# Attention and a two-branch MoE layer on one core: engines ordered by hand, scores in two groups a head pair, q and k loaded as rows of 2 KB

## The chip, the cores and the metric

The kernel runs on one core of a Trainium2 chip. That core has a matrix engine (TensorE, PE in the profile, with its weight loads as PEld), a vector engine (VectorE, DVE), a scalar engine (ScalarE, ACT), GpSimd (POOL) and SyncE (SP), each with its own instruction stream, and 16 DMA engines that they share. TensorE writes its results to PSUM, of which there are eight banks of 128 partitions x 512 f32. The metric is the device time in microseconds (us) of one execution. Three runs of the kernel before took 397.9 us at the median (397.89 to 400.18).

## What is computed

q, k and v have 8 batches, 8 heads, 576 positions and 64 dimensions a head. Attention is causal in blocks of 64, and its output, laid out as 4608 tokens x 512, goes through a layer that takes the greater of two products:

```python
scores = scale * np.matmul(q, k.transpose(0, 1, 3, 2))
mask = block_i >= block_j
scores = np.where(mask, scores, -1000000000.0)
...
attn = attn / (np.sum(attn, axis=-1, keepdims=True) + 1e-09)
return np.matmul(attn, v).astype(np.float32)
...
h1 = x @ w1
h2 = x @ w2
g = np.maximum(h1, h2)
return (g @ w_out).astype(np.float32)
```

w1 and w2 are 512 x 1024, w_out is 1024 x 512. Inputs and output are f32; both kernels compute in bf16 with f32 sums, and leave out the subtraction of the row's maximum.

## The kernel before, in words

**Attention** goes by head pairs: 8 batches of 4 pairs, 32 in all, each done by `attention_pair`. GpSimd issues the loads of q, k and v, which cast to bf16 on the way, in pieces of 64 elements (lines 128, 138 and 142; 12 DMAs a pair with v's last 64 rows apart). TensorE transposes q and k in five chunks of 128 positions (150, 151), both heads at once, so that q^T and k^T hold one head in partitions 0 to 63 and the other in 64 to 127; the results are copied out of PSUM (152, 153). For each chunk of 128 keys the scores of all later queries are computed, transposed (keys in partitions, line 163), the two heads in two matmuls on the two halves of the array. The first chunk has 576 queries and is cut in 512 and 64; so there are six score tiles, which share one PSUM buffer of two banks. ScalarE takes the exponential into a^T (170), and the upper right block of each diagonal tile is set to zero (177). The value matmuls (194) use 128 x 128 pieces of a^T as weights and v with a column of ones as the moving side, 65 columns, 30 a pair. VectorE multiplies by the reciprocal of the ones column's sum (203, 205); TensorE transposes the result (209), and two copies bring it to x^T (213, 217).

**MoE** follows one batch behind for h (`moe_h`) and two behind for y (`moe_y`). h takes, for a batch's 576 tokens, spans of 512 and 64: for each of eight chunks of d_ff and each span four matmuls with w1 (228) and four with w2 (236), so half of the h matmuls have 64 columns. ScalarE (mostly) copies the first product out (244), VectorE takes the maximum with the second (245). y has five tiles of 128 tokens a batch, the last of which overlaps the fourth by 64 tokens, eight matmuls each (253), a copy (261) and a DMA out that GpSimd issues (262).

**What sets the order.** The tile framework's scheduler orders every engine's instructions, and `nc.any` lets it choose the engine of copies and memsets. The code calls attention of pair hp of batch b, then two of the eight h chunks of batch b - 1, then one or two y tiles of batch b - 2. The sixteen weight loads are issued on GpSimd's queue after pair 1 of batch 0. A DMA that GpSimd issues must also wait until the one eight places ahead of it has landed. PSUM has one buffer of two banks for scores, two banks for h and four for everything else.

## Time and profile before

| what | value |
|---|---|
| median of three runs | 397.9 us |
| the profiled execution's span | 399.3 us |
| TensorE matmuls busy | 341.8 us (86%), 3118 recorded |
| VectorE busy | 131.3 us (33%) |
| ScalarE busy | 240.0 us (60%) |
| GpSimd busy, DMA issues included | 252.2 us (63%) |
| software DMA queue | 128192 packets, 28.82 MB, 71.7% of 16 engines |

The times come from one profiled execution. A matmul's time includes the time until its result is through the array, so matmuls that stream one behind the other overlap in the record, and a stretch of busy rows need not be full. What counts there is how far apart the starts are. A row of the timeline gives start, duration of the whole row, engine, source line, operation, tiles written and read, and xN for N instructions in a row; in brackets the idle time before and what ended it.

### The profile page before, as it was taken

The numbers are of one execution on the slowest core, as the hardware profiler recorded it, in microseconds if no ns is written. First come the engines' busy times: TensorE is split into PE (matmuls) and PEld (weight loads), VectorE is DVE, ScalarE is ACT, GpSimd is POOL, SyncE is SP. The second block draws the span as 40 slices with busy tenths as digits, with TensorE's granted clock in tenths as the row PEclk, the third lists the DMA queues.
The fourth block names the chain that finished last, engine by engine and source line by source line (L and its number), as shares of the span: only waits on it lengthen the run. The fifth ranks groups of instructions, "written<-read, shape, count | busy, mean of one in ns | idle before, by whom it ended". The sixth has DMA issues, their size and how long they took to land. (4 is left out here: it accounts for less than half of the span.)

```text
span 399.3 us, 8297 instructions
## 1 busy us (share of the span) xinstructions
PE 341.8 (86%) x3118; PEld 186.6 (47%) x3168; DVE 131.3 (33%) x377; ACT 240.0 (60%) x492; POOL 252.2 (63%) x437
## 2 busy tenths in 40 slices
...
GB/s 53 118 203 110 79 75 48 50 49 48 57 68 76 75 102 76 67 76 66 87 74 75 71 72 71 76 76 100 76 76 71 81 65 28 28 27 29 26 156 83
DMA packets 128232, 29.36 MB, mean 74 GB/s; under 512 B 123584, under 2 KB 124608, under 8 KB 128192
## 3 DMA queue, kind: packets, MB, share of 16 engines
q0 software_dynamic: 128192, 28.82, 71.7%
...
HBM read 36.63 MB, written 10.49 MB: 118 GB/s over the span
## 5 line engine op out<-in xcount | busy, mean ns | idle before, releaser
L170 ACT ACTIVATE aT<-ps_s 128x1024 bf16<-128x1024 f32 (+2 forms) x192 | 118.3, 616 | 48.7 <-PE ps_s L163 46.0
L228 PE MATMUL ps_h<-xT,w_sb 128*128 128x512 bf16 (+1 forms) x505 | 96.2, 289 | 2.8 <-ACT xT L217 1.0
L236 PE MATMUL ps_h<-xT,w_sb 128*128 128x64 bf16 (+1 forms) x496 | 90.5, 286 | 4.3 <-DVE g L245 1.3
L245 DVE TENSOR_TENSOR g<-h1sb,ps_h 128x64 bf16<-128x64 bf16 (+1 forms) x128 | 58.1, 454 | 104.2 <-PE ps_h L236 86.8
L253 PE MATMUL ps_y<-wo_sb,g 128*128 128x512 bf16 x293 | 74.8, 379 | 0.7
L163 PE MATMUL ps_s<-qT,kT 64*128 64x64 bf16 (+4 forms) x384 | 58.8, 299 | 16.6 <-ACT aT L170 9.6
L194 PE MATMUL ps_o<-vv,aT 128*128 128x65 bf16 x960 | 60.8, 202 | 11.5 <-POOL aT L177 9.4
L177 POOL MEMSET aT<- 64x128 bf16 x115 | 23.5, 205 | 73.6 <-ACT aT L170 73.3
L128 POOL DMA_DIRECT2D qn<-in_q_dram x62 | 55.7, 898 | 6.2 <-PE kps L151 3.1
L244 ACT CAST h1sb<-ps_h 128x64 bf16<-128x64 f32 (+1 forms) x115 | 44.5, 387 | 25.0 <-PE ps_h L228 23.3
L138 POOL DMA_DIRECT2D vv<-in_v_dram x64 | 49.7, 777 | 11.7 <-PE ps_o L194 10.7
L194 PEld LDWEIGHTS <-aT 128*128 128x128 bf16 x960 | 44.9, 102 | 25.5 <-POOL aT L177 19.6
L236 PEld LDWEIGHTS <-w_sb 128*128 128x128 bf16 x512 | 37.2, 98 | 39.6 <-issue 18.6
L128 POOL DMA_DIRECT2D kn<-in_k_dram x62 | 55.6, 897 | 0.0
L163 PEld LDWEIGHTS <-kT 64*128 64x128 bf16 x384 | 24.0, 94 | 59.4 <-issue 35.5
L228 PEld LDWEIGHTS <-w_sb 128*128 128x128 bf16 x512 | 38.9, 98 | 25.5 <-issue 4.6
L262 POOL DMA_DIRECT2D out_dram<-ysb x40 | 22.9, 572 | 42.7 <-ACT ysb L261 33.6
L213 ACT COPY xT<-xps 128x512 bf16<-128x512 bf16 x29 | 17.0, 586 | 38.4 <-PE xps L209 38.1
L142 POOL DMA_DIRECT2D vv<-in_v_dram x64 | 37.1, 579 | 0.3 <-issue 0.3
L203 DVE RECIPROCAL rec<-ps_o 128x4 f32<-128x4 f32 (+1 forms) x96 | 17.1, 178 | 61.1 <-PE ps_o L194 60.6
L205 DVE TENSOR_TENSOR xp<-ps_o,rec 128x256 bf16<-128x256 f32 (+1 forms) x96 | 36.3, 378 | 2.2
L253 PEld LDWEIGHTS <-g 128*128 128x128 bf16 x320 | 28.2, 98 | 18.7
...
## 6 DMA issues: line engine op xcount, KB each, us to landing
...
qn<-in_q_dram POOLq DMA_DIRECT2D x62, 80.0 KB, 3.1
kn<-in_k_dram POOLq DMA_DIRECT2D x62, 80.0 KB, 3.1
...
vv<-in_v_dram POOLq DMA_DIRECT2D x64, 8.0 KB, 2.2
...
```

Source lines behind the costliest of these rows:

```text
L128: nc.gpsimd.dma_start(out=dst[:, :, hh, :], in_=flat)
L138: nc.gpsimd.dma_start(out=vv[:, hh, :nfull, :64], in_=vsrc[hh, : nfull * P, :].rearrange("(c p) d -> p c d", p=P),)
L142: nc.gpsimd.dma_start(out=vv[:CH_LAST, hh, nfull, :64], in_=vsrc[hh, nfull * P:, :],)
L163: nc.tensor.matmul(ps[:, hh, :w], kT[hh * BLK:(hh + 1) * BLK, q0:q0 + P], qT[hh * BLK:(hh + 1) * BLK, q0 + st:q0 + st + w], start=True, st ...
L170: nc.scalar.activation(out=aT[:, :, kc, PRE + st:PRE + st + w], in_=ps[:, :, :w], func=AF.Exp, scale=scale,)
L194: nc.tensor.matmul(po[:, gi, hh, :], aT[:, hh, i, cst:cst + P], vv[:, hh, i, :], start=first, stop=(mm == n_mm),)
L205: nc.vector.tensor_mul(xp[:, :ng], po[:, :ng, :, :64], rec[:, :ng].to_broadcast([P, ng, 2, BLK]))
L228: nc.tensor.matmul(ph1[:, :tw], w1_sb[:, dmc, ffc * P:(ffc + 1) * P], xT_sb[:, dmc, ts:ts + tw], start=(dmc == 0), stop=(dmc == n_dmc - 1),)
L236: nc.tensor.matmul(ph2[:, :tw], w2_sb[:, dmc, ffc * P:(ffc + 1) * P], xT_sb[:, dmc, ts:ts + tw], start=(dmc == 0), stop=(dmc == n_dmc - 1),)
L244: nc.any.tensor_copy(out=h1sb[:, :tw], in_=ph1[:, :tw])
L245: nc.vector.tensor_max(g_sb[:, ffc, ts:ts + tw], h1sb[:, :tw], ph2[:, :tw])
L253: nc.tensor.matmul(py[:, :], g_sb[:, ffc, ts:ts + P], wo_sb[:, ffc, :], start=(ffc == 0), stop=(ffc == n_ffc - 1),)
```

## The change

The kernel is written anew under a manual schedule: every engine executes in the order in which the code names the instructions.

- **q and k** are loaded by SyncE as f32, each partition taking eight consecutive positions, 2 KB a head, three pairs ahead (`load_qk`). Two casts on GpSimd a pair bring them to bf16, two pairs ahead (`cast_qk`; those of pairs 0 and 1 are done on VectorE and ScalarE). The transposes are sixteen of 72 columns (`transposes`), whose copies out put the positions in order again; q^T goes out on VectorE, k^T on ScalarE. v is loaded for all eight heads of a batch at once, in five DMAs from GpSimd. Weight loads are eight for w1 and w2 in pieces of 256 columns, issued in pair 0, and two for w_out, issued in pair 1 behind the five v loads of batch 1.
- **Scores** come in two groups, `burst_a` and `burst_b`, with two buffers of two banks. a^T is packed, so that the exponentials are three of 2 x 512 columns and one of 2 x 64. The four mask memsets stay on GpSimd.
- **MoE** works on nine spans of 512 tokens of all 4608, so every h matmul has 512 columns, and y has 36 tiles without overlap. It is a generator: `fill(n)` emits up to n of its matmuls between the parts of a pair (11, 5 and 11), and none if the span's tokens are not done yet; what is left at the end follows the last pair. The h1 copy is always on VectorE, the y copy on ScalarE, the DMA out on SyncE. All tiles but the scores share four PSUM banks.

TensorE in the middle of a steady pair, before: kT and qT are k^T and q^T, ps_s the scores, ps_h a product of the MoE, aT and vv the attention weights and values.

```order
L228 MATMUL ps_h_3004<-xT_109,w_sb 128x512
L163 LDWEIGHTS kT_93
L163 MATMUL ps_s<-qT_92,kT_93 128x64
L163 LDWEIGHTS kT_93
L163 MATMUL ps_s<-qT_92,kT_93 128x64
L228 LDWEIGHTS w_sb
L228 MATMUL ps_h_3004<-xT_109,w_sb 128x512
L194 LDWEIGHTS aT_95
L194 MATMUL ps_o<-vv_94,aT_95 128x65
```

And after, in a steady pair, from the second matmul of the first score tile on:

```order
L241 MATMUL ps_s<-qT_91,kT_93 128x512
L241 LDWEIGHTS kT_93
L241 MATMUL ps_s<-qT_91,kT_93 128x64
L241 LDWEIGHTS kT_93
L241 MATMUL ps_s<-qT_91,kT_93 128x64
L241 LDWEIGHTS kT_93
L241 MATMUL ps_s<-qT_91,kT_93 128x448
L241 LDWEIGHTS kT_93
L241 MATMUL ps_s<-qT_91,kT_93 128x448
L165 LDWEIGHTS w_sb
L165 MATMUL ps_h<-xT,w_sb 128x512
```

Before, each score tile stands between dense matmuls; after, three tiles' matmuls stand together (512, 64 and 448 queries wide) and the next dense matmul comes behind the last.

GpSimd in the program's first pairs, before: the end of the weight loads and the loads of pair 2.

```order
L78 DMA w_sb<-in_moe_w_dram 128x1024
L80 DMA wo_sb<-in_moe_w_out_dram 128x512 x8
L128 DMA qn_102<-in_q_dram 128x5x64
L128 DMA kn_103<-in_k_dram 128x5x64
L138 DMA vv_106<-in_v_dram 128x4x64
L142 DMA vv_106<-in_v_dram 64x64
```

After, from the last mask of pair 0 to the end of what pair 1 gives GpSimd (qraw and kraw are the f32 rows, aT_97 and aT_98 the a^T of pairs 0 and 1):

```order
L280 MEMSET aT_97 64x2x64
L99 CAST qn<-qraw 72x2x8x64
L99 CAST kn<-kraw 72x2x8x64
L118 DMA w_sb<-in_moe_w_dram 128x4x256 x8
L254 MEMSET aT_98 64x2x64 x2
L279 MEMSET aT_98 64x2x64
L280 MEMSET aT_98 64x2x64
L99 CAST qn<-qraw 72x2x8x64
L99 CAST kn<-kraw 72x2x8x64
L108 DMA vv_95<-in_v_dram 128x8x64 x4
L108 DMA vv_95<-in_v_dram 64x8x64
L121 DMA wo_sb<-in_moe_w_out_dram 128x4x512 x2
```

The loads of q and k have left this queue; casts have come, and the masks of pair 1 now stand behind pair 0's casts and weight loads, those of pair 2 behind pair 1's casts and loads.

The core of the diff (what is removed is the code printed above; lines of setup are left out):

```diff
+    CB = [0, 448, 768, 960, 1024]
...
+    ps_s = ctx.enter_context(tc.tile_pool(name="ps_s", bufs=2, space=bass.MemoryType.PSUM))
+    ps_m = ctx.enter_context(tc.tile_pool(name="ps_m", bufs=4, space=bass.MemoryType.PSUM))
...
+    ctx.enter_context(tc.manual_schedule())
...
+    def load_qk(p):
+        b, hp = divmod(p, HP)
+        raws[p] = []
+        for nm, src in (("q", q), ("k", k)):
+            t = raw.tile([P, 2, RPP * D], FP32, name=f"{nm}raw")
+            nc.sync.dma_start(
+                out=t[:NP],
+                in_=src[b, 2 * hp:2 * hp + 2].rearrange("h (p t) d -> p h (t d)", t=RPP),
+            )
+            raws[p].append(t)
+    def cast_qk(p, engines):
+        qk_n[p] = []
+        for nm, t, copy in zip("qk", raws.pop(p), engines):
+            n = qkn.tile([P, RPP, 2, D], BF16, name=f"{nm}n")
+            copy(
+                out=n[:NP].rearrange("p t h d -> p h t d"),
+                in_=t[:NP].rearrange("p h (t d) -> p h t d", d=D),
+            )
+            qk_n[p].append(n)
+    def load_v(b, c):
+        vv = vv_r[b % NV]
+        rows = min(P, S - c * P)
+        nc.gpsimd.dma_start(
+            out=vv[:rows, c, :, :D],
+            in_=v[b, :, c * P:c * P + rows, :].rearrange("h p d -> p h d"),
+        )
...
+    for p in range(3):
+        load_qk(p)
+    load_v(0, 0)
     make_identity(nc, ident)
...
+    for r in range(NV):
+        nc.vector.memset(vv_r[r][:, :, :, D:D + 1], 1.0)
+        nc.vector.memset(vv_r[r][BLK:, NCH - 1, :, :], 0.0)
+    for r in range(NT):
+        nc.vector.memset(kT_r[r][:, S:], 0.0)
+    for r in range(NA):
+        nc.vector.memset(aT_r[r][BLK:, :, CB[4] + 512:], 0.0)
+        nc.vector.memset(aT_r[r][:BLK, :, AW:], 0.0)
+    cast_qk(0, (nc.vector.tensor_copy, nc.scalar.copy))
+    for c in range(1, NCH):
+        load_v(0, c)
+    cast_qk(1, (nc.vector.tensor_copy, nc.vector.tensor_copy))
...
+    pending = []
+    for f in range(4):
+        pending.append(lambda f=f: load_w(w1_sb, w1r, f * 256, 256))
+        pending.append(lambda f=f: load_w(w2_sb, w2r, f * 256, 256))
+    pending += batch_loads(1)
+    pending += [lambda: load_wo(0, 4), lambda: load_wo(4, 4)]
+    LOADS_AT = {0: 8, 1: 9}
...
+    def h_unit(i, f):
+        if f == 0:
+            g_tiles[i] = g_pool.tile([P, NFF, SPAN], BF16, name="g")
+        g = g_tiles[i]
+        t0 = i * SPAN
+        ph = []
+        for w_sb in (w1_sb, w2_sb):
+            pt = ps_m.tile([P, SPAN], FP32, name="ps_h", tag="m")
+            for c in range(NDM):
+                nc.tensor.matmul(
+                    pt[:], w_sb[:, c, f * P:(f + 1) * P], xT[:, c, t0:t0 + SPAN],
+                    start=(c == 0), stop=(c == NDM - 1),
+                )
+                if c == NDM - 1:
+                    if not ph:
+                        h1 = h1_pool.tile([P, SPAN], BF16, name="h1")
+                        nc.vector.tensor_copy(out=h1[:], in_=pt[:])
+                    else:
+                        nc.vector.tensor_max(g[:, f, :], h1[:], pt[:])
+                    ph.append(pt)
+                yield
+    def y_unit(i, s):
+        g = g_tiles[i]
+        t0 = i * SPAN + s * P
+        py = ps_m.tile([P, d_model], FP32, name="ps_y", tag="m")
+        for f in range(NFF):
+            nc.tensor.matmul(
+                py[:], g[:, f, s * P:(s + 1) * P], wo_sb[:, f, :],
+                start=(f == 0), stop=(f == NFF - 1),
+            )
+            if f == NFF - 1:
+                y = y_pool.tile([P, d_model], FP32, name="y")
+                nc.scalar.copy(out=y[:], in_=py[:])
+                nc.sync.dma_start(out=out[t0:t0 + P, :], in_=y[:])
+            yield
+    def moe():
+        ny = SPAN // P
+        for i in range(NSPAN):
+            for f in range(NFF):
+                while done_tokens[0] < (i + 1) * SPAN:
+                    yield False
+                for _ in h_unit(i, f):
+                    yield True
+                if i > 0 and f % 2 == 0:
+                    for _ in y_unit(i - 1, f // 2):
+                        yield True
+        for s in range(ny):
+            for _ in y_unit(NSPAN - 1, s):
+                yield True
...
+    def transposes(p):
+        b, hp = divmod(p, HP)
+        tiles = []
+        for nm, src in zip("qk", qk_n.pop(p)):
+            pt = ps_m.tile([P, RPP, NP], BF16, name=f"ps_{nm}T", tag="m")
+            for j in range(RPP):
+                nc.tensor.transpose(
+                    pt[:, j, :], src[:NP, j].rearrange("p h d -> p (h d)"), ident[:NP, :NP],
+                )
+            t = (qT_r if nm == "q" else kT_r)[p % NT]
+            dst = t[:, :S].rearrange("q (p j) -> q p j", j=RPP)
+            sv = pt.rearrange("q j p -> q p j")
+            if nm == "q":
+                nc.vector.tensor_copy(out=dst, in_=sv)
+            else:
+                nc.scalar.copy(out=dst, in_=sv)
+            tiles.append(t)
+        st[p] = tiles
...
+    def scores(p, ps, col, c, q0, w, m=P):
+        qT, kT = st[p]
         for hh in range(2):
...
+            r = slice(hh * D, (hh + 1) * D)
+            nc.tensor.matmul(
+                ps[:m, hh, col:col + w], kT[r, c * P:c * P + m], qT[r, q0:q0 + w],
+                start=True, stop=True,
+            )
...
+    def burst_a(p):
+        u0 = ps_s.tile([P, 2, 512], FP32, name="ps_s", tag="s")
+        scores(p, u0, 0, 0, 0, 512)
+        u1 = ps_s.tile([P, 2, 512], FP32, name="ps_s", tag="s")
+        scores(p, u1, 0, 0, 512, 64)
+        scores(p, u1, 64, 1, 128, 448)
+        exp(p, u0, 512, 0)
+        mask(p, 0)
+        exp(p, u1, 512, 512)
+        mask(p, 576)
+    def burst_b(p):
+        u2 = ps_s.tile([P, 2, 512], FP32, name="ps_s", tag="s")
+        scores(p, u2, 0, 2, 256, 320)
+        scores(p, u2, 320, 3, 384, 192)
+        u3 = ps_s.tile([P, 2, 512], FP32, name="ps_s", tag="s")
+        scores(p, u3, 0, 4, 512, 64)
+        exp(p, u2, 512, 1024)
+        nc.gpsimd.memset(aT_r[p % NA][BLK:, :, 1024:1088], 0.0)
+        nc.gpsimd.memset(aT_r[p % NA][BLK:, :, 1344:1408], 0.0)
+        exp(p, u3, 64, 1536, m=BLK)
...
+        rec = small.tile([P, 3, 2, 1], FP32, name="rec")
+        nc.vector.reciprocal(rec[:, :n, :, 0], po[:, :, :, D])
+        xp = xpool.tile([P, 3, 2, D], BF16, name="xp", tag=f"xp{n}")
+        nc.vector.tensor_mul(
+            xp[:, :n], po[:, :, :, :D], rec[:, :n].to_broadcast([P, n, 2, D])
         )
...
+    def x_out(p):
+        b, hp = divmod(p, HP)
+        _, _, x01, x234 = st.pop(p)
+        pt = ps_m.tile([P, NCH, P], BF16, name="ps_x", tag="m")
+        for t in range(NCH):
+            src = x01[:, t] if t < 2 else x234[:, t - 2]
+            nc.tensor.transpose(pt[:, t, :], src.rearrange("p a d -> p (a d)"), ident[:])
+        px = pt.rearrange("p t w -> p (t w)")[:, :S]
+        nc.vector.tensor_copy(out=xT[:, hp, b * S:(b + 1) * S], in_=px)
+        if hp == HP - 1:
+            done_tokens[0] = (b + 1) * S
+    transposes(0)
+    for p in range(NPAIR):
+        b, hp = divmod(p, HP)
+        burst_a(p)
+        fill(11)
+        burst_b(p)
+        if p + 3 < NPAIR:
+            load_qk(p + 3)
+        if p + 2 < NPAIR:
+            cast_qk(p + 2, (nc.gpsimd.tensor_copy, nc.gpsimd.tensor_copy))
+        if hp == 0 and 1 <= b < B - 1:
+            pending += batch_loads(b + 1)
+        for _ in range(LOADS_AT.get(p, 2)):
+            if pending:
+                pending.pop(0)()
+        av(p, [0, 1])
+        if p + 1 < NPAIR:
+            transposes(p + 1)
+        fill(5)
+        av(p, [2, 3, 4])
+        fill(11)
+        x_out(p)
+    while next(moe_steps, None) is not None:
+        pass
```

## Rows read from the trace of the kernel before

**Rows 1.** Windows by stage: stretch, its length, then busy time by engine.
```profile
core 0: us, PE busy (x) PEld busy (x) DVE busy (x) ACT busy (x) POOL busy (x), PEclk, DMA share, GB/s
0.00:58.40 58.40, 26.71 (x217) 15.67 (x221) 8.61 (x36) 26.06 (x54) 50.04 (x76) 1.00 1.17 108
58.40:98.60 40.20, 35.30 (x359) 19.27 (x362) 20.28 (x55) 23.27 (x48) 27.71 (x48) 1.00 0.77 50
98.60:357.70 259.10, 245.86 (x2350) 135.88 (x2386) 95.00 (x270) 178.03 (x364) 168.53 (x302) 1.00 0.70 69
357.70:394.50 36.80, 33.95 (x204) 15.75 (x206) 7.41 (x17) 12.63 (x26) 5.97 (x11) 1.00 0.21 79
```

**Rows 2.** Timeline of TensorE in one steady pair of batch 4.
```profile
197.25 0.38 PE L236 MATMUL ps_h<-xT,w_sb 128*128 128x512 bf16 x1
197.56 0.39 PE L163 MATMUL ps_s<-qT,kT 64*128 64x512 bf16 x2
197.88 0.82 PE L236 MATMUL ps_h<-xT,w_sb 128*128 128x512 bf16 x3
...
203.74 0.62 PE L194 MATMUL ps_o<-vv,aT 128*128 128x65 bf16 x14
...
205.51 1.03 PE L253 MATMUL ps_y<-wo_sb,g 128*128 128x512 bf16 x4
206.38 0.22 PE L150 MATMUL qps<-ident,qn 128*128 128x128 bf16 x1
206.43 0.22 PE L151 MATMUL kps<-ident,kn 128*128 128x128 bf16 x1
```

**Rows 3.** Timeline of GpSimd in the first 30 us.
```profile
0.28 0.11 POOL L296 MEMSET const-float32-1.0<- 128x1 f32 x1
...
2.04 0.31 POOL masks.py:199 TENSOR_SCALAR_AFFINE_SELECT ident<-ident 128x128 bf16<-128x128 bf16 x1
2.28 0.91 POOL L128 DMA_DIRECT2D qn<-in_q_dram  x1
...
4.06 0.77 POOL L138 DMA_DIRECT2D vv<-in_v_dram  x1
...
7.27 0.60 POOL L142 DMA_DIRECT2D vv<-in_v_dram  x1
...
13.94 0.66 POOL L77 DMA_DIRECT2D w_sb<-in_moe_w_dram  x1
...
28.16 0.53 POOL L80 DMA_DIRECT2D wo_sb<-in_moe_w_out_dram  x1 [0.72 <-DMA w_sb<-in_moe_w_dram]
```

**Rows 4.** Timeline of TensorE in pair 4, early.
```profile
66.07 1.91 PE L236 MATMUL ps_h<-xT,w_sb 128*128 128x512 bf16 x4
```

**Rows 5.** Groups by line and shape: busy us, mean ns of one, idle before.
```profile
L245 DVE TENSOR_TENSOR g<-h1sb,ps_h 128x512 bf16<-128x512 bf16 x64 | 44.0, 688 | 91.4 <-PE ps_h L236 74.2 <-PE ps_s L163 14.7 <-ACT h1sb L244 2.1
...
L170 ACT ACTIVATE aT<-ps_s 128x1024 bf16<-128x1024 f32 x32 | 32.8, 1025 | 3.8 <-PE ps_s L163 3.8
...
L205 DVE TENSOR_TENSOR xp<-ps_o,rec 128x256 bf16<-128x256 f32 x64 | 27.0, 422 | 1.3
...
L177 POOL MEMSET aT<- 64x128 bf16 x115 | 23.5, 205 | 73.6 <-ACT aT L170 73.3
...
L152 ACT COPY qT<-qps 128x640 bf16<-128x640 bf16 x32 | 22.1, 692 | 19.0 <-PE qps L150 19.0
...
L153 DVE COPY kT<-kps 128x640 bf16<-128x640 bf16 x29 | 14.3, 492 | 65.7 <-PE kps L151 65.7
...
L203 DVE RECIPROCAL rec<-ps_o 128x4 f32<-128x4 f32 x64 | 11.7, 183 | 60.6 <-PE ps_o L194 60.3
...
L102 DVE MEMSET vv<- 64x130 bf16 x3 | 0.5, 167 | 0.3
```

**Rows 6.** DMA issues: count, KB each, us from issue to landing.
```profile
qn<-in_q_dram POOLq DMA_DIRECT2D x62, 80.0 KB, 3.1
```

**Rows 7.** Timeline of TensorE, the last y matmuls.
```profile
377.88 13.98 PE L253 MATMUL ps_y<-wo_sb,g 128*128 128x512 bf16 x63
```

More of the change, by code (lines that the diff above doesn't have):

```diff
@@ L249, in moe_y @@
-    def moe_y(b, g_sb, subs):
-        for ts in subs:
-            py = psum_sm.tile([P, 512], FP32, name="ps_y", tag="pssm")
-            for ffc in range(n_ffc):
-                nc.tensor.matmul(
-                    py[:, :],
-                    g_sb[:, ffc, ts:ts + P],
-                    wo_sb[:, ffc, :],
-                    start=(ffc == 0),
-                    stop=(ffc == n_ffc - 1),
-                )
-            ysb = ysb_pool.tile([P, 512], FP32, name="ysb")
-            nc.any.tensor_copy(out=ysb[:, :], in_=py[:, :])
-            nc.gpsimd.dma_start(
-                out=out[b * S + ts:b * S + ts + P, :], in_=ysb[:, :]
-            )
@@ new lines @@
+    ctx.enter_context(tc.manual_schedule())
+    NV, NA, NT = 3, 3, 2
+    qT_r = [ring.tile([P, S], BF16, name=f"qT{r}") for r in range(NT)]
+    kT_r = [ring.tile([P, S + APAD], BF16, name=f"kT{r}") for r in range(NT)]
+    vv_r = [ring.tile([P, NCH, H, D + 1], BF16, name=f"vv{r}") for r in range(NV)]
+    aT_r = [ring.tile([P, 2, AW + APAD], BF16, name=f"aT{r}") for r in range(NA)]
+    xT = ring.tile([P, NDM, NTOK], BF16, name="xT")
+    w1_sb = wpool.tile([P, NDM, d_ff], BF16, name="w1_sb")
@@ new lines @@
+    w2_sb = wpool.tile([P, NDM, d_ff], BF16, name="w2_sb")
+    wo_sb = wpool.tile([P, NFF, d_model], BF16, name="wo_sb")
+    ident = wpool.tile([P, P], BF16, name="ident")
+    raws = {}
+    qk_n = {}
+    def load_qk(p):
[8 more added lines that the diff above has]
+            raws[p].append(t)
@@ new lines, in fill @@
+    def fill(n):
+        for _ in range(n):
+            if not next(moe_steps, False):
+                return
+    st = {}
+    def transposes(p):
[16 more added lines that the diff above has]
+        st[p] = tiles
@@ new lines, in scores, with exp, mask @@
+    def scores(p, ps, col, c, q0, w, m=P):
+        qT, kT = st[p]
+        for hh in range(2):
+            r = slice(hh * D, (hh + 1) * D)
[3 more added lines that the diff above has]
+            )
+    def exp(p, ps, w, a0, m=P):
+        nc.scalar.activation(
+            out=aT_r[p % NA][:m, :, a0:a0 + w], in_=ps[:m, :, :w], func=AF.Exp, scale=scale,
+        )
+    def mask(p, a0, n=1, step=0):
+        a = aT_r[p % NA]
+        if n == 1:
+            nc.gpsimd.memset(a[BLK:, :, a0:a0 + BLK], 0.0)
+        else:
+            nc.gpsimd.memset(
+                a[BLK:, :, a0:a0 + n * step].rearrange("p h (n s) -> p h n s", s=step)[:, :, :, :BLK],
+                0.0,
+            )
```

250 lines of the change are left out of this document (46 added, 204 removed).

## The prediction

> **What bounds the kernel now.** I read the windows by stage first, because the shares over the whole span mix three stages with different limits. [rows 1] cuts the profiled 399.3 us at the starts of attention pair 4 (58.4, where the first dense MoE work begins), of batch 2 (98.6), at the end of attention (357.7), and at the last output's issue. The reader should see that TensorE is busy 27 of the first 58 us, and 246 of the 259 us in which six batches run, 43.2 us each. There TensorE is the bound, but busy is not streaming, since a matmul's row includes its fill.
>
> So next the timeline of one pair [rows 2], for spacings. Four 512-column matmuls in a row take 1.03 us and one takes 0.38, so they follow each other at 0.217. Transposes of 128 columns start 0.055 apart, and 14 value matmuls of 65 columns in 0.62 give about 0.032. The two score matmuls of a pair of heads run beside each other: both of 512 columns end after 0.39. But the scores start 0.31 after a single 512-column matmul, and the next dense matmul 0.32 after them, where 0.217 would do. Each run of scores thus costs 0.1 us going in and 0.1 coming out. There are six runs in a pair, 24 in a batch.
>
> A steady batch at these spacings (0.00042 us a column): 40 transposes 2.2, scores 4 x 1600 columns 2.7, 120 value matmuls 3.8, 20 output transposes 1.1, h 64 x 0.217 + 64 x 0.03 = 15.8, y 40 x 0.217 = 8.7. Together 34.3 of 43.2 us. Of the 8.9 us lost, 24 x 0.2 = 4.8 are the score runs; the other 4.1 are waits for PSUM tiles and masks.
>
> The start is another limit. GpSimd issues every transfer: 0.6 to 0.9 us for each piece of q, k and v, then sixteen weight loads, the last eight of which wait for earlier ones to land, until 28.7 us [rows 3]. Only then come loads of pairs 2, 3 and 4. TensorE is also slow there: four 512-column matmuls take 1.91 us at 66 us [rows 4] against 1.03 later, so it runs at the 1.2 GHz level, though the windows print a granted clock of 1.00 for all stages.
>
> **The change, part by part.**
>
> *Steady batches (2 to 7).* Per pair there are now 16 transposes of 72 columns (0.033 each, between 0.032 and 0.055), the same scores, value and output work, and at most 27 MoE matmuls, all of 512 columns. An MoE span may start only when its tokens are done, so a batch holds one span: 64 h and 32 y matmuls, 27 + 27 + 27 + 15 over its pairs. Stream: 2.1 + 2.7 + 3.8 + 1.1 + 96 x 0.217 = 30.5. Scores come in two runs a pair: 8 x 0.2 = 1.6. In the fourth pair nothing is left to fill between the last value matmuls and the output transposes, so reciprocal, multiply (at most 1.5 x 0.42, [rows 5]) and two handovers stand bare, 1.1. In the other three, the second value group reuses the PSUM bank of k^T, which ScalarE copies out (at most 0.69) behind four exponentials. Counting from a pair's start: scores 0.65, eleven MoE matmuls to 3.0, scores to 3.5, exponential of 1.03 to 4.45, the short one to 4.75, k^T copy to 5.4, against TensorE ready at 5.3 (value group 0.2, transposes 0.53, five matmuls 1.1 after 3.5). I take 0.3 each. A batch: 30.5 + 1.6 + 1.1 + 0.9 = 34.1, six 204.6 against 259.1. **-54.5.** From below 32.1 (no wait); from above 39.6 (the 2.3 us a pair lost now are all lost again).
>
> *VectorE and ScalarE.* The h1 copies go from ScalarE to VectorE: 16 tile operations a batch, at most 0.69 each, 11.1 us. With four times 2.6 for a pair's own work (two copies 0.5 to 0.7, reciprocals 0.36, multiplies 0.42 and 0.63) VectorE has some 21.5 of 34.1 us, so nothing waits for its rate. Three exponentials of 1.03 and a short one replace six; with the k^T and y copies ScalarE has some 5 us a pair. Output DMAs and q, k loads move to SyncE, which does nothing now. q and k are loaded three pairs ahead, about 25 us, against 3.1 us to land [rows 6]. I cost these at nothing.
>
> *GpSimd casts.* Two a pair, 72 partitions x 1024 f32 to bf16; no row shows one. Nearest rows: a memset of 128 elements 0.20 and an affine select of 128 in 0.31 [rows 3, 5], a memset of one element about 0.11. Taking that 0.11 as the fixed part, 0.7 to 1.6 ns an element, so 0.9 to 1.7 us; with no fixed part 2.5. I take 1.3, near the middle of the first two. GpSimd then has 0.8 (four memsets) + 2.6 + 1.3 (value loads, 1.1 each for 1024 pieces, by 0.60 for 64, 0.77 for 512 and 0.91 for 640) = 4.7 us a pair. Queued behind the casts and loads are the next pair's masks, for which the value matmuls wait: GpSimd gets free for casts at 4.9 of an 8.9 us pair and masks are wanted 3.5 into the next, so 7.5 us are there for casts and two loads. Up to 2.6 us a cast the masks are in time. For ordinary elementwise work the Trainium skill (GPSIMD Engine Reference, "Performance versus the Vector engine") advises VectorE and measures 2.6 cycles an element on GpSimd, with two inputs; by that a cast would be an estimated 2.2 us and the sum below 348. No run here shows it yet.
>
> *Start.* Value load landed at about 4.0, memsets that wait for it on VectorE 2.8 (three of 64 x 520 by 0.167 for 130), q cast 1.2, transposes and copy with two more casts ahead of it: first scores at 11.4 (10.4 now). With no fill and at the low clock a pair takes 7.5: scores 0.7, exponentials to 4.1, second value group to 5.8, normalisation and output transposes to 7.5. Pair 0 ends at 18.9. GpSimd then holds up pairs 1 and 2: two casts and eight weight loads of 512 pieces (0.77 each) keep it from 15.7 to 24.5, so pair 1's masks come 4 us late and pair 2 starts at 29.1; two casts, five value loads and two output-weight loads, which wait for earlier weight loads, keep it from 25.3 to about 36. Pair 3 starts at 40.5, **pair 4 at 48 instead of 58.4: -10.4**. Bounds: 44 (casts 0.9, loads landing early) and 57 (casts 2.5, and weight loads in 512-byte rows at twice the time assumed).
>
> *Batch 1.* Pair 4 has 8 us at half clock: 12.9. Pair 5: 8.95. MoE may do only 64 matmuls in this batch, so pair 6 gets ten and pair 7 none: 7.5 and 6.3. With 1.4 for lower clock 37.0 against 40.2: **-3.2** (33 to 44).
>
> *Tail.* Deferred work: two spans and their last y, 224 matmuls x 0.217 = 48.6. Now 357.7 to the last matmul at 391.9, 34.2 [rows 1, 7]. **+14.4.** From the last matmul to the end of the span 7.4 us, as now.
>
> Sum: 399.3 - 54.5 - 10.4 - 3.2 + 14.4 = 345.6, against the profiled execution. The median run is 1.4 us below that execution, so **344.**
>
> **Rivals.**
> 1. *The waits stay.* In-order engines and one pool of four banks for six kinds of tile: each pair keeps the 2.3 us lost now, and a batch takes 39.6. Then 345.6 + 33 - 1.4 = 377. For it: 4.1 us of today's loss are such waits. Against: most MoE matmuls are placed where something is awaited.
> 2. *GpSimd becomes the bound (the slower side).* Past 3.2 us a cast, GpSimd has more work in a pair than TensorE, masks come late, and a pair takes 2.1 + 2 casts. With X a cast: start 48 + 4(X - 1.3), 28 pairs of 2.1 + 2X, tail 48.6 and 7.4: 158 + 60X. That meets 398 at X = 4.0, 3.9 ns an element, 1.6 times the highest bound; at 4.5 it is 428.
> 3. *The clock falls.* Today it stays up once dense work has begun. Pairs 6 and 7 now leave TensorE idle half the time, and the fourth pair of each batch for 1 us. If it falls to the 1.2 GHz level in batch 1, some 6.5 us more, 350; if in every batch, about 5 us six times, 374. The Trainium skill (TensorE: Matmul & The Clock Gate, "HAM oscillation") says that pauses between bursts bring the low clock back, and the early rows at half speed agree with it; whether pauses this short do, no row shows.
> 4. *Everything fits.* Start 44, batch 1 33, batches 32.5: 328.
>
> **How the numbers follow.** Forecast 0.60 (own range 334 to 357), waits stay 0.15, clock in every batch 0.07, all fits 0.10, GpSimd bound 0.05, something unseen 0.03. The range 328 to 374 leaves out rival 2 and the worse halves of 1 and 3. Faster by over 1% 0.92, within 1% (what a measurement can tell from no change) 0.02, slower 0.06.
>
> **What would show it.** In the new profile: windows with pair 4's scores at 48, batches of 34, about 49 us of dense 512-column matmuls at the end; two score runs a pair, 0.1 at each edge; casts at 0.9 to 2.5 us; the largest TensorE wait for the k^T copy, not for a mask. The forecast is wrong if casts exceed 3.2 us, if 512-column matmuls go back to 0.43 spacing after batch 1, or if value matmuls wait over 1 us a pair.

## The result, and the profile after

The changed kernel takes **342.5 us** (median of four runs, 338.9 to 344.1) against 399.0 in the runs of before beside it: a ratio of **0.850, 95% interval 0.845 to 0.856**. The ratios and intervals here and below are of fast runs alone; of the changed kernel's four runs that leaves out the two at 344. The forecast was 344. The profiled execution is the fastest of the four, and in it TensorE's granted clock never falls once it has risen; in the other three its mean is 0.985 to 0.989, and what that costs is told below. By the stages of [rows 1]:

| stage | before | forecast | profile after |
|---|---|---|---|
| to pair 4's scores | 58.4 | 48.0 | 54.7 |
| batch 1 | 40.2 | 37.0 | 31.3 |
| batches 2 to 7 | 259.1 | 204.6 | 198.9 |
| deferred MoE | 34.2 | 48.6 | 48.3 |
| last matmul to end | 7.4 | 7.4 | 3.9 |
| span | 399.3 | 345.6 | 337.1 |

So the time was met by errors of both signs: the start is 6.7 us longer than forecast, everything else shorter. The profiled execution is 8.5 us below the forecast's sum of 345.6; that the median comes within 2 us of the forecast is luck, for in most executions the clock fell for a while, some 4 us that the sum leaves out. The windows of the changed kernel at these bounds, with the start cut again at its first scores (stretch, length, busy us of PE, PEld, DVE, ACT and POOL with counts, PEclk, DMA share, GB/s), as [rows 1]:

```profile
0.00:19.90 19.90, 1.14 (x16) 0.98 (x17) 5.12 (x18) 2.97 (x3) 5.08 (x11) 1.00 0.96 150
19.90:54.70 34.80, 21.17 (x254) 14.74 (x254) 9.47 (x23) 14.55 (x20) 22.42 (x39) 1.00 1.36 191
54.70:86.00 31.30, 27.64 (x317) 15.06 (x316) 20.34 (x40) 14.60 (x20) 14.95 (x29) 1.00 0.60 78
86.00:284.90 198.90, 194.08 (x2076) 105.01 (x2075) 121.07 (x240) 99.69 (x143) 82.92 (x166) 1.00 0.57 107
```

In the six batches TensorE is busy 194 of 199 us. The stretch from first scores to pair 4 is 34.8 us, nearly the 36.6 forecast; it is the 19.9 ahead of it that was not.

One steady pair on TensorE (batch 3), and the end of a fourth pair, as [rows 2] (start, us, engine, line, operation, tiles, count, idle before and its releaser):

```profile
152.27 0.61 PE L241 MATMUL ps_s<-qT,kT 64*128 64x512 bf16 x6
152.81 1.90 PE L165 MATMUL ps_h<-xT,w_sb 128*128 128x512 bf16 x8
154.55 0.81 PE L183 MATMUL ps_y<-wo_sb,g 128*128 128x512 bf16 x3
155.29 0.42 PE L241 MATMUL ps_s<-qT,kT 64*128 64x320 bf16 x6
...
155.84 0.43 PE L224 MATMUL ps_qT<-ident,qn 72*128 72x72 bf16 x8
...
156.36 1.25 PE L183 MATMUL ps_y<-wo_sb,g 128*128 128x512 bf16 x5
157.44 0.89 PE L295 MATMUL ps_o<-vv,aT 128*128 128x65 bf16 x24
158.17 2.54 PE L165 MATMUL ps_h<-xT,w_sb 128*128 128x512 bf16 x11
...
184.21 0.27 PE L314 MATMUL ps_x<-ident,xp 128*128 128x128 bf16 x2
185.25 0.34 PE L314 MATMUL ps_x<-ident,xp 128*128 128x128 bf16 x3 [0.77 <-DVE xp L303]
```

Two score runs a pair; 72-column transposes; no wait on the second value group (157.44), where I had put 0.3 us for the k^T copy; and in the fourth pair the bare normalisation, two output transposes, 0.77 us of wait, three more. A batch is 33.1 to 33.3 us.

The start, by the rows that carry it, two of VectorE's and four of GpSimd's, as [rows 3]:

```profile
13.44 0.09 DVE L129 MEMSET vv<- 128x40 bf16 x1 [13.44 <-DMA vv<-in_v_dram]
17.35 1.22 DVE L99 CAST qn<-qraw 72x1024 bf16<-72x1024 f32 x2
...
23.88 1.03 POOL L99 CAST qn<-qraw 72x1024 bf16<-72x1024 f32 x1
25.84 5.96 POOL L118 DMA_DIRECT2D w_sb<-in_moe_w_dram  x8
31.84 0.34 POOL L254 MEMSET aT<- 64x128 bf16 x2
...
43.35 0.34 POOL L254 MEMSET aT<- 64x128 bf16 x2
```

VectorE's first memset of a value buffer waits until 13.4 us for the first value load, and q's first cast stands behind all memsets. Later the masks of pairs 1 and 2 (31.84, 43.35) stand behind the issue of eight and seven loads, as forecast. A GpSimd cast is 1.03 us.

### The profile page after: what moved, and what is told of

It reads as the page before. It is cut to its first block, busy times and chain, and to the rows that moved or that the text cites. A ratio compares the mean times of both kernels' runs of the same rounds, so it can differ in the third digit from the quotient of the medians.

```text
span 337.1 us, 7097 instructions
## 1 busy us (share of the span) xinstructions
PE 292.4 (87%) x2880; PEld 157.5 (47%) x2880; DVE 178.5 (53%) x353; ACT 138.8 (41%) x198; POOL 125.4 (37%) x244
## 2 busy tenths in 40 slices
DMA packets 57984, 36.63 MB, mean 109 GB/s; under 512 B 39008, under 2 KB 44128, under 8 KB 57952
## 3 DMA queue, kind: packets, MB, share of 16 engines
q0 software_dynamic: 42784, 7.87, 31.5%
## 4 chain that ended last, share of the span: by engine, by line
PE 80%; DMA 7%; issue 4%; DVE 3%; ACT 2%; POOL 2%; POOLq 0%; ACTq 0%
PE ps_h L165 37%; PE ps_y L183 18%; PE ps_o L295 10%; PE ps_s L241 7%; DMA w_sb<-in_moe_w_dram 4%; DMA vv<-in_v_dram 4%; PE ps_x L314 3%; PE ps_qT L224 2%; PE ps_kT L224 2%; ACT aT L247 2%; DVE xp L303 2%; POOL w_sb L118 1%; DVE rec L301 1%; DVE vv L130 0%; POOL qn L99 0%
## 5 line engine op out<-in xcount | busy, mean ns | idle before, releaser
L247 ACT ACTIVATE aT<-ps_s 128x1024 bf16<-128x1024 f32 (+1 forms) x128 | 99.2, 831 | 120.1 <-PE ps_s L241 119.1
L165 PE MATMUL ps_h<-xT,w_sb 128*128 128x512 bf16 x576 | 139.2, 381 | 0.0
L165 PEld LDWEIGHTS <-w_sb 128*128 128x128 bf16 x576 | 52.3, 98 | 60.7 <-issue 6.2
L172 DVE CAST h<-ps_h 128x512 bf16<-128x512 f32 x72 | 49.6, 689 | 43.9 <-PE ps_h L165 43.5
L174 DVE TENSOR_TENSOR g<-h,ps_h 128x512 bf16<-128x512 bf16 x72 | 49.5, 687 | 13.3 <-PE ps_h L165 12.1
L241 PE MATMUL ps_s<-qT,kT 64*128 64x64 bf16 (+4 forms) x384 | 37.0, 296 | 6.2 <-ACT aT L247 5.5
L108 POOL DMA_DIRECT2D vv<-in_v_dram x40 | 33.8, 852 | 11.8 <-DVE vv L129 11.0
L303 DVE TENSOR_TENSOR xp<-ps_o,rec 128x256 bf16<-128x256 f32 x64 | 31.4, 491 | 2.2
L99 POOL CAST qn<-qraw 72x1024 bf16<-72x1024 f32 x30 | 31.2, 1039 | 1.9
L99 POOL CAST kn<-kraw 72x1024 bf16<-72x1024 f32 x30 | 31.3, 1043 | 0.0
L233 ACT COPY kT<-ps_kT 128x576 bf16<-128x576 bf16 x32 | 20.1, 628 | 22.0 <-PE ps_kT L224 21.9
```

The lines of the kernel that those rows point to most:

```text
L99: copy(out=n[:NP].rearrange("p t h d -> p h t d"), in_=t[:NP].rearrange("p h (t d) -> p h t d", d=D),)
L108: nc.gpsimd.dma_start(out=vv[:rows, c, :, :D], in_=v[b, :, c * P:c * P + rows, :].rearrange("h p d -> p h d"),)
L165: nc.tensor.matmul(pt[:], w_sb[:, c, f * P:(f + 1) * P], xT[:, c, t0:t0 + SPAN], start=(c == 0), stop=(c == NDM - 1),)
L172: nc.vector.tensor_copy(out=h1[:], in_=pt[:])
L174: nc.vector.tensor_max(g[:, f, :], h1[:], pt[:])
L241: nc.tensor.matmul(ps[:m, hh, col:col + w], kT[r, c * P:c * P + m], qT[r, q0:q0 + w], start=True, stop=True,)
```

## The experiments

x1 to x5, x7 and x8 change one thing of the changed kernel; x6 adds to x5, x9 to x6, x10 and x11 to x7. Ratios are to the kernel before, beside which each ran. "Steady batch" is the distance of the first scores of batches 3 to 7.

| run | us, median | ratio (95%) | first scores | pair 4 | batch 1 | steady batch |
|---|---|---|---|---|---|---|
| changed kernel | 342.5 | 0.850 (0.845–0.856) | 19.9 | 54.7 | 31.3 | 33.2 |
| x1 six score runs | 367.8 | 0.920 (0.916–0.924) | 19.0 | 54.7 | 34.2 | 37.1 |
| x2 fill in one lump | 380.6 | 0.951 (0.945–0.957) | 18.7 | 54.1 | 36.4 | 38.7 |
| x3 casts twice | 345.7 | 0.864 (0.859–0.868) | 21.9 | 58.9 | 33.9 | 33.2 |
| x4 casts four times | 420.3 (one run) | 1.05 | 21.5 | 68.7 | 43.1 | 42.3 |
| x5 start: memsets first | 343.4 | 0.858 (0.855–0.862) | 10.4 | 55.2 | 33.3 | 33.2 |
| x6 and loads spread | 340.3 | 0.844 (0.836–0.852) | 10.6 | 52.0 | 33.3 | 33.2 |
| x7 even fill | 335.5 | 0.839 (0.834–0.843) | 20.6 | 55.8 | 32.6 | 32.0 |
| x8 casts on VectorE | 350.5 | 0.877 (0.873–0.880) | 21.1 | 57.7 | 34.2 | 34.0 |
| x9 v read as rows | 339.9 | 0.850 (0.846–0.854) | 10.7 | 52.8 | 33.6 | 33.2 |
| x10 even, y in own batch | 334.3 | 0.834 (0.831–0.837) | 19.0 | 56.4 | 35.7 | 32.9 |
| x11 even, y partly | 335.4 | 0.838 (0.837–0.839) | 19.1 | 54.2 | 35.6 | 32.7 |
| x12 ordered loads | 323.7 | 0.808 (0.806–0.809) | 8.6 | 43.4 | 28.7 | 32.0 |

**What do the score runs cost, and what does the place of the fill do?** (x1, x2)

```diff
 scores(p, u0, 0, 0, 0, 512)
+fill(1)            # the same after three more score calls, and
 ...                # 9 and 3 instead of 11 and 5 elsewhere
```

> The changed kernel, with one MoE matmul placed between the score calls of a pair, so that its ten score matmuls stand in six runs again instead of two; the number of MoE matmuls in a pair stays at 27. Theory (each run of scores costs 0.1 us going in and 0.1 coming out): four more runs a pair are 0.8 us, 3.2 a batch; six steady batches 19, batch 1 about 2, so +21 us on the changed kernel, a steady batch of 36.3 instead of 33.1, some 363 us, 0.90 of the time before. Rival (the gaps at the runs of the old kernel were waits for banks and exponentials, not a cost of the edge): no more than +4 us, 346, 0.86.

The first half of a pair of x1 on TensorE, columns as above:

```profile
164.88 0.39 PE L241 MATMUL ps_s<-qT,kT 64*128 64x512 bf16 x2
165.20 0.39 PE L165 MATMUL ps_h<-xT,w_sb 128*128 128x512 bf16 x1
165.52 0.20 PE L241 MATMUL ps_s<-qT,kT 64*128 64x64 bf16 x2
165.66 0.39 PE L165 MATMUL ps_h<-xT,w_sb 128*128 128x512 bf16 x1
165.98 0.36 PE L241 MATMUL ps_s<-qT,kT 64*128 64x448 bf16 x2
```

No row has a wait, and yet a score run of 512 columns and the single MoE matmul behind it start 0.32 us apart each, where 0.217 would stream them: 0.10 at each edge, 0.21 a run. The batch is 4.0 us longer for 16 more runs, 0.25 each. In four steady batches TensorE's rows name 4.3 us of waits, against 3.1 in the changed kernel; without these 1.2 us it is 0.23 each. The edge's price is there without any wait, and that rival is out; the price is the 0.2 I took, or a little more.

```diff
 burst_a(p)
-fill(11)
+fill(27)           # and no fill at the two later places
```

> The changed kernel, with all 27 MoE matmuls of a pair in one place, between the two score bursts, instead of 11, 5 and 11. Theory (the fill's places are the cover of the exponentials, masks and normalisation): after the second burst the second value group waits some 0.4 us for the second exponential and its mask, and the output transposes about 1.0 for reciprocal and multiply; the fourth pair has the latter bare already. Per batch 3 x 1.4 + 0.4 = 4.6, six batches and part of batch 1 about +30 us, a steady batch of 37.7, 372 us, 0.93. Rival (TensorE's total work sets the time, and four banks let it run ahead wherever the fill stands): under +6 us, 348, 0.87.

Waits of TensorE in steady batches 3 to 6 of x2 (us in total, times, longest):

```profile
PE ps_x L314 <- DVE xp L303: 12.3, 16, 0.8
PE ps_o L295 <- POOL aT L279: 2.7, 6, 0.8
PE ps_o L295 <- DVE xp L303: 2.6, 12, 0.2
```

The normalisation lies bare in all 16 pairs, and some value groups wait for masks too. The batch grows by 5.5 us (4.6 expected). The waits named here are 4.4 us a batch, against 0.8 in the changed kernel: 3.6 of the 5.5, the rest no row names. The same matmuls in another place lose more than half of what the change won in a batch.

**Is GpSimd near the path?** (x3, x4, x8)

```diff
+for _ in range(2 if p > 1 else 1):     # x4: 4
     copy(out=n[:NP]..., in_=t[:NP]...)
```

> The changed kernel, with each of GpSimd's q and k casts done twice, so 2.1 us where one takes 1.04. Theory (GpSimd stays clear of the bound up to 2.6 us a cast): steady batches unchanged at 33.1 to 33.5; only the start is later, since the casts of pairs 2, 3 and 4 stand ahead of masks there, +2 to +6 us, so 345 to 349, 0.87. Rival (GpSimd is already close to the path, its loads and masks being uncounted): 2.1 us more a pair show up in every batch, +8 each, 400 us, 1.00.

> The changed kernel, with each of GpSimd's q and k casts done four times, 4.2 us. By the formula of the slower rival, 158 + 60X with X = 4.17, the time is 408 us, a pair takes 10.4 us, TensorE's waits for masks on GpSimd come to about 2 us a pair, and TensorE's first stage ends some 12 us later. If masks have more slack than the formula gives (value groups wait late, or the casts overlap the loads' issue), 360 to 385.

At 2.1 us a cast the steady batch is unchanged to 0.1 us and pair 4 starts 4.2 later. Of these, 2.0 are there at the first scores, ahead of any doubled cast: in the versions with the start's code unchanged these come at 18.7 to 21.9. At 4.2 the formula of rival 2 holds for a pair: 10.6 us against 10.4. Of the 12 us by which 420 lies over 408, 9 are the start's (pair 4 at 68.7, by the formula at 59.5). GpSimd is busy 157 of 169 us in four batches, and TensorE waits for masks:

```profile
155.30:324.60 169.30, 138.45 (x1396) 75.14 (x1396) 81.75 (x160) 68.40 (x96) 157.34 (x212) 0.95 0.52 94
```
```profile
PE ps_o L296 <- POOL aT L255: 27.8, 14, 3.6
```

The changed kernel, at 1.04, is clear of that by a factor of two or more.

```diff
-cast_qk(p + 2, (nc.gpsimd.tensor_copy, nc.gpsimd.tensor_copy))
+cast_qk(p + 2, (nc.vector.tensor_copy, nc.vector.tensor_copy))
```

> The changed kernel, with the q and k casts of pair 2 and later on VectorE (0.65 us each) instead of GpSimd (1.04). Theory (VectorE has 121 of 199 us in the steady batches, so 1.3 a pair more fits; GpSimd's masks in pairs 1 to 3 come 2 us earlier each): steady batches 33.2 to 33.8, start 2 to 5 us earlier, 338 to 343, 0.85. Rival (two casts stand in VectorE's queue just ahead of the reciprocal and the q^T copy, and hold up the pair): +0.5 to 1.3 us a pair, 356 to 378, 0.89 to 0.94.

Neither fits. The steady batch is 34.0, 0.8 longer and just past the range, and the start is later, not earlier. VectorE and TensorE in a fourth pair of x8:

```profile
191.16 0.68 DVE L99 CAST qn<-qraw 72x1024 bf16<-72x1024 f32 x1
...
192.36 0.17 DVE L301 RECIPROCAL rec<-ps_o 128x4 f32<-128x4 f32 x1
...
194.17 0.19 DVE L301 RECIPROCAL rec<-ps_o 128x6 f32<-128x6 f32 x1
...
192.97 0.89 PE L295 MATMUL ps_o<-vv,aT 128*128 128x65 bf16 x24 [0.43 <-ACT kT L233]
195.01 0.34 PE L314 MATMUL ps_x<-ident,xp 128*128 128x128 bf16 x3 [1.03 <-DVE xp L303]
```

The casts stand ahead of the reciprocal in VectorE's queue, and all that follows there is late just where no fill covers it: the output transposes wait 1.03 us instead of 0.77. In four steady batches the waits that TensorE's rows name come to 6.5 us against 3.1, which is the 0.8 a batch. The value group's 0.43 for the k^T copy, which stands there once, these rows don't explain. At the start GpSimd, free of casts, runs into its own queue: it waits for weight loads to land, 3.8 us ahead of the last wo load, and the masks of pair 2 stand behind that until 46.3 (43.35 in the changed kernel, whose first scores came 1.2 us earlier). The Trainium skill (GPSIMD Engine Reference, "Engine selection") gives elementwise work to VectorE, and says that on GpSimd work with one input is roughly at line rate. The trace agrees with both on the instruction: 0.69 us on VectorE (the mean of the 63 casts in x8) against 1.04, and the latter about 1 ns an element. The kernel is slower all the same, 8 us by the medians and 6 against the two runs of the changed kernel with nearly the same mean granted clock (344.0 and 344.1, 0.985 against 0.984): the choice of engine was one of queues.

**What sets the start?** (x5, x6, x9)

```diff
-load_v(0, 0); make_identity(nc, ident)
-for r in range(NV): memsets of vv_r[r]
+make_identity(nc, ident); memsets of vv_r[0]
+cast_qk(0, ...); load_v(0, 0..4); memsets of vv_r[1], vv_r[2]
```

> The changed kernel, with the first value buffer's memsets, and then q's cast on VectorE, ahead of the value loads; the other value buffers' memsets come after. In the changed kernel VectorE's first memset waits until 13.4 us for the first value load, and the first scores come at 19.9 us. Theory (that wait alone made the start later than forecast): k's first load has landed by 6.2 us, so first scores at 8 to 9, and pair 4 starts 7 to 11 us earlier than 54.7, at 44 to 48; the time is 332 to 336, 0.83. Rival (the transfers of the first 50 us, at 7 to 9 tenths of the DMA engines, set the start wherever the order on VectorE puts it): first scores early, but pair 4 still at 52 to 55, 340, 0.85.

```diff
-LOADS_AT = {0: 8, 1: 9}
+LOADS_AT = {0: 4, 1: 4, 2: 3}     # on top of x5
```

> As the kernel with the memsets and the cast first, and with GpSimd's weight and value loads spread 4, 4, 3, 2 over the first pairs instead of 8 and 9 in pairs 0 and 1. Theory (in pairs 1 and 2 masks stand behind the issue of loads, 4 to 6 us each): a further 5 to 9 us, pair 4 at 37 to 42, 325 to 330, 0.82. Rival (DMA engines busy at 9 tenths set the start): no gain over the kernel without the spread, pair 4 within 2 us of it.

My first theory fell here. With the wait of 13.4 us gone, first scores come at 10.4, and pair 4 no earlier. TensorE in pair 0 of x5, and ten value loads' times to landing in x5, then in the changed kernel:

```profile
17.12 0.32 PE L299 MATMUL ps_o<-vv,aT 128*128 128x65 bf16 x3 [3.83 <-DMA vv<-in_v_dram]
26.35 0.32 PE L299 MATMUL ps_o<-vv,aT 128*128 128x65 bf16 x3 [8.91 <-DMA vv<-in_v_dram]
...
29.92 0.98 PE L299 MATMUL ps_o<-vv,aT 128*128 128x65 bf16 x15 [0.85 <-DMA vv<-in_v_dram]
```
```profile
DMA to landing us min/median/max: 7.7/12.1/25.7
```
```profile
DMA to landing us min/median/max: 3.6/11.4/12.0
```

Pair 0's value groups wait for one value chunk after another, until 29.9. The DMA engines' busy tenths in x5, in slices of 8.6 us, stand at the top until pair 4:

```profile
DMA  9999996584067458546865487448744000011013
```

Spreading GpSimd's loads (x6) gives 3.3 us at pair 4, not the 5 to 9 expected, since pair 0 still ends at 31. Page part 3 of the changed kernel shows what pieces cost (queue, packets, MB, share of 16 engines):

```profile
q0 software_dynamic: 42784, 7.87, 31.5%
q1 hardware_dynamic: 15168, 28.32, 29.0%
```

31.5% of 16 x 337.1 us over 42784 packets is 40 ns for one of 184 bytes; on the queue of q, k and outputs it is 103 ns for one of 1.9 KB. These are means over a queue; in the trace the values' own pieces, 36864 of 128 bytes, take 36 ns each, and the pieces of 2 KB 112. A batch's values are 4608 pieces, so an estimated 10 us of all 16 engines; a pair's q and k, 288 pieces, 2.0. In x5 SyncE had issued six pairs' q and k by 9.7 us, around these values: it runs ahead as far as the raw buffers let it, whatever pair TensorE is in. The Trainium skill (DMA: Bandwidth & Descriptors, "Rules for kernel authors") says that spreading transfers over issuing engines does not help bandwidth, as all use the same 16 DMA engines and interleave. The trace agrees: in x5, with both queues in use, batch 0's values landed at 17.1 to 30.3, though issued by 5.3, against 13.2 to 21.8 in the changed kernel.

```diff
-in_=v[b, :, c * P:c * P + rows, :].rearrange("h p d -> p h d")
+in_=(the same bytes from whole rows).rearrange("(p h d) -> p h d")   # on x6
```

> As the kernel with the start's memsets first and its loads spread, but every value load reads the same number of bytes from whole rows of 2 KB, 128 pieces instead of 1024. The values then land in the wrong places: the transfer of v in its own order is what is left out. There value chunks landed 7.7 to 25.7 us after their issue, and pair 0's value group waited until 26 us for one. Theory (the small pieces of v fill the DMA engines and set the start): chunks land within 6 us, pair 0 ends at 18 to 21, pair 4 starts at 40 to 44 instead of 52.0, the time is 328 to 333, 0.82 to 0.83. Rival (the bytes of q, k, v and the weights, or GpSimd's issue, set it): pair 4 at 50 to 53, 338 to 341, 0.845.

This one told nothing of the pieces: the page counts 57984 packets, 39008 of them under 512 B, as in every other run, so the transfers were still cut by head. Its times repeat those of x6.

**What is left in a batch, and the clock** (x7, x10, x11)

```diff
-fill(11) ... fill(5) ... fill(11)
+fill(10) ... fill(4) ... fill(10)
```

> The changed kernel, with 10, 4 and 10 MoE matmuls at the three places of a pair instead of 11, 5 and 11, so that the fourth pair of a batch gets 24 too instead of 15. Theory (the bare normalisation of the fourth pair, 0.77 us waited and about as much at its value group, is the one wait left in a steady batch): TensorE's waits for the normalised tile vanish from batch 2 on, a steady batch takes 32.2 to 32.5 instead of 33.2, six of them -4 to -6 us, so 337, 0.84. Rival (4 and 10 are too few to cover k^T's copy and the exponentials in the other three pairs): the wait moves to the value groups, within 1 us of no change, 342.

As expected, a little more: 1.2 us a steady batch and 7.0 in all (5.9 between the two runs that kept the clock throughout, 333.0 and 338.9), and no wait of TensorE for the normalised tile from batch 2 on. With no wait left that a row of TensorE names in batches 3 to 6, the forecast's stream of 30.5 leaves 0.19 for each of the eight runs in a steady batch of 32.0.

In the profiles of eight versions (x1 to x9 without x4) the granted clock fell to half for some 7 to 10 us around pair 7, which has no fill. TensorE in that pair of x5, whose order from pair 4 on is the changed kernel's, and in the same pair of the changed kernel's profiled execution:

```profile
83.34 0.40 PE L245 MATMUL ps_s<-qT,kT 64*128 64x320 bf16 x4 [0.96 <-ACT aT L251]
...
84.75 0.67 PE L228 MATMUL ps_qT<-ident,qn 72*128 72x72 bf16 x8
```
```profile
81.89 0.39 PE L241 MATMUL ps_s<-qT,kT 64*128 64x320 bf16 x4 [0.96 <-ACT aT L247]
...
83.17 0.42 PE L224 MATMUL ps_qT<-ident,qn 72*128 72x72 bf16 x8
```

The same wait of 0.96 us, and once eight transposes take 0.67 behind them, once 0.42. So after the same pauses the clock falls in one execution and not in another; the changed kernel's own four runs have mean granted clocks of 1.00 once and 0.985 to 0.989 three times. In x5, pair 7 and batch 2 take 1.1 and 2.8 us more than in the changed kernel's profile: 3.8 us. That would be most of the 5.2 that lie between the four runs of the result, only one of which has a trace.

```diff
 y_unit(i, s) for all s right after span i's h (x10)
 span 0 so, later spans with two y tiles late (x11)
 12 (x10) or 8 (x11) of 16 h1 copies on ScalarE
```

> The evenly filled kernel, in which a span's 32 y matmuls come right after its 64 h matmuls, in the same batch, instead of among the next span's; 12 of 16 h1 copies a batch are on ScalarE to share the drains. Batch 1 so has 96 MoE matmuls instead of 64 and the tail 192 instead of 224. Theory (in the profiles of eight other versions TensorE's granted clock fell to half for 7 to 10 us around 84 to 97 us, when pairs 6 and 7 had little fill; filled, they keep it): no record at half between 60 us and the end, batch 1 at 32 to 33.5, the tail 41.2 instead of 48.1, 327 to 331, 0.82 to 0.83. Rival (without y among them, h tiles come faster than VectorE and ScalarE empty the four banks): a steady batch of 34 or more, 340 or more.

> The evenly filled kernel, in which span 0's y is all done in batch 1, and of each later span two y tiles in its own batch and two among the next span's h; 8 of 16 h1 copies a batch are on ScalarE. Batch 1 has 96 MoE matmuls, batch 2 has 80, the tail 208. Theory: clock kept in batch 1, steady batches 32.0 to 32.3, tail 44.7, 329 to 333, 0.825 to 0.835. Rival (the clock falls in batch 1 whatever fills it, or batch 2's thinner fill takes its place): at least one record at half and 334 to 337, the time of the evenly filled kernel.

Filled, pairs 6 and 7 keep the clock in both (mean granted clock 1.00 in their profiles, no fall from pair 5 to the end). So the theories' part on the clock held, and the times missed their ranges (327 to 331 and 329 to 333). Batch 1 takes 3 us more than in x7 for its 32 more matmuls, which in x10 saves 7 us in the tail. The gain is lost in the steady batches, longer by 0.7 (x11) to 0.9 (x10), of which the waits that TensorE's rows name are 0.2; the rest stays open. Both end within 1.2 us of x7.

**A version that beats both** (x12)

```diff
-for p in range(3): load_qk(p)          # raw buffers: 4
+load_qk(0); memsets of vv_r[0]; cast_qk(0, ...); load_v(0, 0..4); ...
+transposes(0); load_qk(1); cast_qk(1, ...); load_qk(2)   # raw buffers: 2
-LOADS_AT = {0: 8, 1: 9}
+LOADS_AT = {0: 2, 1: 2, 2: 3, 3: 3, 4: 3, 5: 2, 6: 3}   # v of batch 1 third
-fill(11) ... fill(5) ... fill(11)
+fill(10) ... fill(4) ... fill(10)      # pairs 4 to 7: 6, 4, 6
```

> Four things at once: fill of 10, 4, 10 from batch 2 on; in batch 1 its 64 MoE matmuls in equal parts, 6, 4, 6 a pair, instead of first come; the start's memsets first; and the loads in the order in which they are needed: q, k of pair 0, the values of batch 0, then q, k of pairs 1 and 2 (two raw buffers each instead of four, so that SyncE can't run ahead), the first two weight pieces, the values of batch 1, the other weights. Theory (the transfers' time on the DMA engines sets the start, and what they carry first is of choice): value chunks of batch 0 have landed by 17 to 21 us instead of 26 to 28, pair 4 starts at 43 to 48; with 16 matmuls in every pair the clock holds from pair 5 on, batch 1 takes 27 to 30; steady batches 32.0; together 316 to 323 us, 0.79 to 0.81. Rival (all transfers together, and not their order, set the start): pair 4 at 51 to 55 or pair 4's value groups wait for v, 326 to 332, 0.82 to 0.83. If the clock falls in the thinner fill, batch 1 takes 34 or more and records at half stand in pairs 5 to 7.

323.7 us, 0.7 above its own range and 5% under the changed kernel. Times to landing of the same ten value loads; on TensorE's timeline pair 0's last value group, and pair 8's second one with the h matmuls behind it; windows of batches 1, 2 and 3 to 7:

```profile
DMA to landing us min/median/max: 5.6/7.3/16.0
```
```profile
20.20 1.10 PE L298 MATMUL ps_o<-vv,aT 128*128 128x65 bf16 x15 [3.64 <-DMA vv<-in_v_dram]
...
80.76 0.61 PE L298 MATMUL ps_o<-vv,aT 128*128 128x65 bf16 x15 [3.41 <-DMA vv<-in_v_dram]
...
81.68 3.55 PE L168 MATMUL ps_h<-xT,w_sb 128*128 128x512 bf16 x8
```
```profile
43.40:72.20 28.80, 27.53 (x313) 15.08 (x320) 19.25 (x39) 14.79 (x20) 19.24 (x35) 1.00 1.26 181
72.20:109.40 37.20, 33.46 (x343) 18.06 (x348) 20.75 (x41) 16.91 (x24) 15.98 (x31) 0.95 0.76 113
109.40:269.40 160.00, 158.20 (x1698) 87.63 (x1727) 102.50 (x200) 84.02 (x119) 67.41 (x136) 1.00 0.58 113
```

With the values early, pair 0's last value group comes at 20.2 instead of 29.9, and pair 4 at 43.4: 8.5 us better than x6 with the same transfers in another order. Of these, 2.0 are there at the first scores and 6.5 come in pair 0; pairs 1 to 3 take 6.9 to 7.0 each in both. That answers x5's question for order against volume, though of order it doesn't tell apart fewer q and k ahead of the values and fewer weights in pair 0. Batch 1's equal parts give 28.7 us and keep the clock. Batch 2 alone misses: its last value chunk was ordered too late, a value group waits 3.41 us for it, and the clock is at half for the 3.4 us that follow, eight h matmuls in 3.55 us instead of 1.9. The batch is 37.2 instead of 32.0. That chunk a pair earlier would be the next thing to do; it was not tried.

## Why the prediction was right, and where by luck

- **Steady batches: right in mechanism, 5.7 us too long in six.** Taken were 30.5 stream + 1.6 edges + 1.1 normalisation + 0.9 k^T. The k^T wait is not there: no such wait stands in a steady batch of the changed kernel. The bare normalisation is 0.77 (x7: 1.2 with all that hangs on it). A score run costs 0.19 (x7, as what is left over) to 0.25 (x1, with its waits). 30.5 + 8 x 0.25 + 0.77 is 33.3 and 30.5 + 8 x 0.19 + 1.2 is 33.2, both as measured: how the 2.7 us divide between the two these runs leave open.
- **Where the 10 us a batch came from** was forecast as 3.8 stream, 3.2 edges and the waits. x1 gives 3.7 to 4.0 for the edges, without and with the waits in it. x2 shows that where the fill stands is worth 5.5, so it is the fill's places that kept the waits (4.1 in the old kernel) from coming back. Rival 1 is out. Its 39.6 us a batch was also too high by its own terms: the 8.9 us that it brings back hold 4.8 of edges, of which the change keeps 1.6. With the 4.1 of waits it would be 36.2, still 3 us above the measured batch.
- **GpSimd:** forecast 1.3 a cast, measured 1.04, near the lower bound. x3 bears out the slack, and x4 rival 2's formula for a pair. The 2.2 us that I worked out from the Trainium skill (GPSIMD Engine Reference, "Performance versus the Vector engine") was from a figure for two inputs and did not hold for a cast, which has one.
- **Start: the step that failed.** I let the first value load land at about 4.0 us, by the 3.1 of [rows 6]. That row was measured with one queue at work. With SyncE's q and k of the first four pairs issued by 3.9 us it took until 13.4. From there to the first scores it is 6.5 us, where I had 7.4, and pairs 0 to 3 take 34.8 against 36.6: the landing alone made the start late. I had costed the move of q and k to SyncE at nothing, with landing times of before. That it was the transfers and not VectorE's wait is shown by x5 and x12. (The kernel before issues eight loads a pair, and twelve for the last pair alone, not twelve for each as its description says.)
- **Batch 1: 31.3 against 37.0, below its lower bound of 33.** Of the 5.7 us some 4 are clock. I had given pair 4 8 us at half, and 1.4 more for lower clock later. Its first 11 h matmuls already mix both levels, and the next 11 run in full:

```profile
55.66 3.58 PE L165 MATMUL ps_h<-xT,w_sb 128*128 128x512 bf16 x11
...
62.22 2.54 PE L165 MATMUL ps_h<-xT,w_sb 128*128 128x512 bf16 x11
```

Pair 4 takes 10.3 instead of 12.9, and pairs 6 and 7 6.6 and 5.7 instead of 7.5 and 6.3. That holds for the profiled execution; x3 and x5 to x7, where the clock falls in pair 7, have 32.6 to 33.9. So rival 3 came true in its small form in most executions, at about 4 us, and not in every batch.
- **Tail:** 48.3 against 48.6, 224 matmuls at 0.216. **End:** 3.9 against 7.4. By the traces, GpSimd issued the last output 1.4 us after its copy was done (392.53 to 393.94) and SyncE issues it at once (333.90 to 333.93); where the other 2 us went was not tested.
